# Decode attention with a gated MLP: K and V in 4 MB tiles, small operands as single rows, late weights in a K buffer, and h as a row

## The chip, the cores and the metric

The kernel runs on one core of one Trainium2 chip. The metric is device time in microseconds (us), the median of several executions. The time includes about 1.8 us beyond the span that the profile shows: the profiled execution of the old kernel took 193.56 us with a span of 191.8 us. The profile is of one execution. In it PE is the matrix engine (TensorE), PEld its weight loads, DVE the vector engine, ACT the scalar engine, SP the engine that issues most DMAs. This chapter calls an execution slow when it is over 1.5% above the fastest of the same kernel, and the comparisons of kernels use fast executions, except where it says so. The runs were made on several chips; each is compared with the old kernel on its own chip.

## The reference, cut to what matters

```
x = A_x                                             # [1, 1, 512], bf16
g = sigmoid((x * gate_w).sum(-1))
q = (x @ wq) as 32 heads of 128                     # wq: 4 MB
p = softmax(q . k_cache * 128**-0.5)                # 32 heads, 4096 keys: K 32 MB
a = (p . v_cache) as one row of 4096 @ wo           # V 32 MB, wo 4 MB
h = max(x @ w1 + b1, 0) ** 2                        # w1: 512 x 1376, 1.4 MB
b = h @ w2 + b2                                     # w2: 1376 x 512, 1.4 MB
out = g * a + (1 - g) * b                           # 512 numbers
```

One token reads 78 MB and computes little. Whatever order the work takes, those bytes have to cross the DMA engines.

## The kernel before

K and V come in sixteen tiles of 2 MB each, two heads to a tile, and every partition receives one run of 16 KB. K has four buffers, V three.

```
NP = 16;  NB = 64;  HB = NB // 2;  NK, NV = 4, 3;  PG = 4
k_t = A_k_cache ... .rearrange("(t p f) -> t p f", p=128, f=NB * 128)

d_wq = P.dma("sp", "wq", ... wbig <- wq)            # runs of 32 KB for each partition
d_x  = P.dma("act", "x",  ... x4   <- x  spread as [128, 4])    # 128 packets of 8 bytes
d_gw = P.dma("act", "gw", ... gw4  <- gate_w spread alike)
d_b1, d_b1r, d_b2 = ...                             # b1 in packets of 20 and 2 bytes
```

DVE multiplies half a K tile by q. Each key then has 128 products: PE, with an identity as its weights, adds their eight groups of 16, DVE adds up the 16 sums that are left, ACT takes the exponential, and PE multiplies by V:

```
for c in range(n):                                  # 8 matmuls for each half tile
    matmul(red[i % 2], ident, v[:, c, :, :], start=(c == 0), stop=(c == n - 1))
```

At the end the weights w1, wo, w2 arrive behind the last V tile, in this order. h is computed as columns, with w1 as the stationary operand, the one that is loaded into PE as weights (44 small matmuls of one column each), and everything is accumulated straight into one tile out_ps of PSUM, the memory that takes PE's results, so that after the last w2 matmul only one DVE copy and the store remain:

```
for j in range(32): to_out(wo_v[:, j, :], op_sb[:, j:j+1], ...)        # 64 matmuls of 256 columns
to_out(w2_r, ...)
for n, (lo, hi) in enumerate(W2_CUTS):              # ((0, 6), (6, 9), (9, 10)): three DMAs
    for j in range(lo, hi): done = to_out(w2_sb[:, j, :], hs[:, j:j+1], ...)
f = tensor_copy(fin, out_ps)
```

The softmax here doesn't subtract the row's maximum and nothing guards it: scores larger than these inputs give would overflow.

## Time and profile before

| | old kernel |
|---|---|
| median time | 194.76 us (194.51 to 194.91, 3 executions) |
| span of the profiled execution | 191.8 us |
| read from HBM | 78.32 MB |
| DMA rate from 20 to 170 us | 427 to 428 GB/s |
| last weights land (end of the last data packet in the trace) | 188.5 us |
| from there to the end of the span | 3.3 us |

The page of the old kernel: its first line, and the DMA share (tenths) and GB/s in 40 equal slices.

```profile
span 191.8 us, 1729 instructions
...
DMA  6999999999999999999999999999999999999991
GB/s 219 438 383 380 434 427 420 427 427 431 437 424 427 420 431 424 437 427 427 424 431 422 437 427 419 424 431 431 431 431 424 417 434 431 434 414 434 434 346 43
```

The engines that move data are busy from the second slice to the last but one. The third and fourth slices (383 and 380) are lower than the rest.

The table by windows of the old kernel: the window and its length, busy time and number of instructions for each engine, the granted PE clock (1.00 is full speed), the mean busy share of the 16 DMA engines, GB/s.

```profile
20.00:50.00 30.00, 17.50 (x87) 6.22 (x88) 19.97 (x18) 1.42 (x9) 0.00 (x0) 0.77 1.01 428
50.00:80.00 30.00, 20.11 (x126) 7.50 (x124) 19.90 (x14) 3.35 (x17) 0.00 (x0) 0.89 1.01 428
80.00:110.00 30.00, 19.01 (x112) 7.10 (x104) 17.26 (x12) 2.68 (x13) 0.00 (x0) 0.83 1.01 428
110.00:140.00 30.00, 19.47 (x104) 6.30 (x99) 17.35 (x12) 2.22 (x13) 0.00 (x0) 0.83 1.01 427
140.00:170.00 30.00, 18.74 (x104) 6.88 (x103) 17.17 (x12) 2.54 (x13) 0.00 (x0) 0.83 1.00 427
```

PE and DVE are busy for 17 to 20 of every 30 us, while the DMA share is full. Compute waits for data here, not the other way round. The Trainium skill, "DMA: Bandwidth & Descriptors", section Bandwidth, puts the ceiling of the path into SBUF at 435 GB/s; the 427 to 428 measured here is 98% of it.

The last pieces of the chain of waits of the old kernel, that is of the work that ended last, followed back from the end through what each piece waited for (start, length, what):

```profile
153.35 35.32 DMA w_sb<-in_B_w_dram
...
188.71 0.62 PE out_ps L354 x8
189.36 0.42 DVE fin L385
```

The last eight matmuls wait for their weights and then take 0.62 us. TensorE keeps up with the weights to the end.

One line of the list of DMA issues (size, and us from issue to landing):

```profile
x<-in_A_x_dram ACTq DMA_DIRECT2D x1, 1.0 KB, 12.8
```

One kilobyte takes 12.8 us, as long as the 4 MB of wq. The same page of the skill, section "Queues, rings and completion order", says that a DMA engine alternates between its queues packet by packet. The trace agrees: x lands together with wq, its tiny packets spread over wq's 10 us.

### The profile page before, as it was taken

How to read it: one execution, taken by the hardware profiler on the slowest of the kernel's cores; microseconds unless marked ns; L12 is line 12 of the kernel's file. 1: busy time of each engine (PE TensorE's matmuls, PEld its weight loads, DVE VectorE, ACT ScalarE, POOL GpSimd, SP SyncE). 2: the span in 40 equal slices, each digit the busy share in tenths (PEclk: the TensorE clock that was granted, in tenths of full speed). 3: DMA queues.
4: the chain of work that ended last, by engine and by line, in shares of the span. 5: the costliest groups of instructions: out<-in, count | busy, mean ns of one | idle time of the engine just before them, and what ended most of it. 6: DMA issues, size and time to landing. Idle time of an engine off the chain costs nothing.

```text
span 191.8 us, 1729 instructions
## 1 busy us (share of the span) xinstructions
PE 114.5 (60%) x721; PEld 45.6 (24%) x721; DVE 96.5 (50%) x83; ACT 17.3 (9%) x74; POOL 3.1 (2%) x13
## 2 busy tenths in 40 slices
PE   0009006998849493719573938484776654685974
PEld 0004002333212321303132312121232121223742
DVE  2000009699965655647473838382929191921300
ACT  2003100011102010101020101010111010102000
POOL 6000000000000000000000000000000000000000
PEclk9999955699996969985999696969697899579588
DMA  6999999999999999999999999999999999999991
GB/s 219 438 383 380 434 427 420 427 427 431 437 424 427 420 431 424 437 427 427 424 431 422 437 427 419 424 431 431 431 431 424 417 434 431 434 414 434 434 346 43
DMA packets 6285, 78.42 MB, mean 409 GB/s; under 512 B 1187, under 2 KB 1414, under 8 KB 1670
## 3 DMA queue, kind: packets, MB, share of 16 engines
q1 hardware_dynamic: 5732, 78.32, 97.0%
q8 instruction: 5, 0.08, 0.2%
q10 hardware_dynamic: 546, 0.01, 0.2%
q14 instruction: 2, 0.02, 0.0%
HBM read 78.32 MB, written 0.00 MB: 408 GB/s over the span
## 4 chain that ended last, share of the span: by engine, by line
DMA 77%; DVE 10%; PE 8%; SPq 2%; ACTq 1%; issue 1%
DMA Vt<-in_A_v_cache_dram 28%; DMA w_sb<-in_B_w_dram 18%; DMA Kt<-in_A_k_cache_dram 17%; DMA b_sb<-in_B_b_dram 13%; DVE prod L238 8%; PE red L252 5%; PE qps L279 3%; DVE S L259 2%; SPq L324 1%; SPq L322 0%; ACTq L164 0%; SPq L233 0%; PE out_ps L354 0%; DVE b_g L217 0%; ACTq L162 0%
## 5 line engine op out<-in xcount | busy, mean ns | idle before, releaser
L252 PE MATMUL red<-prod,ident 128*128 128x512 bf16 x256 | 74.1, 442 | 42.6 <-DVE prod L238 42.6
L238 DVE TENSOR_TENSOR prod<-Kt,qb 128x4096 bf16<-128x4096 bf16 x32 | 73.1, 2285 | 43.4 <-DMA Kt<-in_A_k_cache_dram 43.4
L252 PEld LDWEIGHTS red<-prod,ident 128*128 128x128 bf16 x256 | 25.2, 108 | 88.6 <-DVE prod L238 50.9
L259 DVE TENSOR_REDUCE S<-red 128x32 f32<-128x512 f32 x32 | 22.0, 686 | 8.5 <-PE red L252 8.4
L279 PE MATMUL qps<-Vt,E 128*32 128x512 bf16 x256 | 22.0, 476 | 4.7 <-DMA Vt<-in_A_v_cache_dram 3.1
L267 ACT ACTIVATE E<-S 64x64 bf16<-64x64 f32 x32 | 8.8, 274 | 131.7 <-DVE S L259 131.5
L197 PE MATMUL qps<-wbig,xb 128*64 128x512 bf16 x32 | 5.0, 480 | 14.0 <-DVE xb L188 14.0
L279 PEld LDWEIGHTS qps<-Vt,E 128*32 128x32 bf16 x256 | 6.4, 109 | 20.6 <-issue 16.7
L220 PE MATMUL out_ps<-b_g,ones 1*64 1x256 f32 x4 | 1.1, 656 | 9.8 <-DVE b_g L217 9.8
L188 DVE COPY xb<-x 128x512 bf16<-128x512 bf16 x1 | 0.4, 427 | 11.4 <-DMA x<-in_A_x_dram 11.4
L197 PEld LDWEIGHTS qps<-wbig,xb 128*64 128x64 bf16 x32 | 2.2, 135 | 16.3 <-DVE xb L188 14.0
L354 PE MATMUL out_ps<-wbig,op_sb 128*1 128x256 bf16 x64 | 5.3, 335 | 1.3 <-DMA wbig<-in_A_wo_dram 1.3
L267 ACT ACTIVATION_READ_ACCUMULATOR E<-S 64x1 f32 x32 | 5.9, 185 | 0.0
L217 DVE TENSOR_SCALAR b_g<-b_sb,gate 1x512 f32<-1x512 bf16 x1 | 0.5, 475 | 8.5 <-DMA b_sb<-in_B_b_dram 8.5
L291 PEld LDWEIGHTS o_ps<-pick,acc_sb 128*128 128x128 f32 x32 | 4.1, 191 | 1.6 <-ACT acc_sb L286 1.2
L291 PE MATMUL o_ps<-pick,acc_sb 128*128 128x8 f32 x32 | 3.9, 249 | 0.7 <-ACT acc_sb L286 0.7
L385 DVE CAST fin<-out_ps 128x256 bf16<-128x256 f32 x1 | 0.4, 425 | 7.2 <-PE out_ps L354 7.2
L354 PEld LDWEIGHTS out_ps<-wbig,op_sb 128*1 128x1 bf16 x64 | 3.1, 101 | 3.2 <-DMA wbig<-in_A_wo_dram 1.6
L201 ACT ACTIVATE qb<-qps 128x512 bf16<-128x512 f32 x4 | 2.4, 598 | 12.3 <-PE qps L197 12.3
L286 ACT ACTIVATE acc_sb<-qps 128x512 f32<-128x512 f32 x4 | 2.4, 597 | 10.2 <-PE qps L279 10.2
L210 DVE TENSOR_SCALAR gate<-gate 128x1 f32<-128x1 f32 x1 | 0.2, 154 | 5.9 <-ACT gate L209 5.9
L220 PEld LDWEIGHTS out_ps<-b_g,ones 1*64 1x64 f32 x4 | 0.3, 199 | 9.9 <-DVE b_g L217 9.9
(40 smaller groups left out, 18.8 us busy)
## 6 DMA issues: line engine op xcount, KB each, us to landing
Kt<-in_A_k_cache_dram SPq DMA_DIRECT2D x16, 2048.0 KB, 31.6
Vt<-in_A_v_cache_dram SPq DMA_DIRECT2D x16, 2048.0 KB, 27.3
wbig<-in_A_wq_dram SPq DMA_DIRECT2D x1, 4096.0 KB, 12.6
wbig<-in_A_wo_dram SPq DMA_DIRECT2D x2, 2048.0 KB, 32.2
w_sb<-in_B_w_dram SPq DMA_DIRECT2D x1, 1376.0 KB, 25.3
w_sb<-in_B_w_dram SPq DMA_DIRECT2D x1, 768.0 KB, 34.8
w_sb<-in_B_w_dram SPq DMA_DIRECT2D x1, 384.0 KB, 35.3
w_sb<-in_B_w_dram SPq DMA_DIRECT2D x1, 128.0 KB, 34.1
```

The costliest lines, as they stand in the source:

```text
L197: last = P.add("pe", lambda e, c=c, half=half, t=t: e.matmul(qps[c % 2][64 * half:64 * half + 64, :], xb[:, t, 0:64], wq_v[:, t, 4 * c:4 * ...
L201: q_done.append(P.add("act", lambda e, c=c: e.activation(qb[:, 4 * c:4 * c + 4, :], qps[c % 2][:, :].rearrange("p (g d) -> p g d", d=128), ...
L220: P.add("pe", lambda e, hh=hh: e.matmul(out_ps[64 * hh:64 * hh + 64, :], ones[0:1, 0:64], b2_g[0:1, 256 * hh:256 * hh + 256], start=True, ...
L238: prods[p, half] = P.add("dve", lambda e: e.tensor_tensor(prod[:, i % 2, :].rearrange("p (b d) -> p b d", d=128), Kt[:, p % NK, half * HB ...
L252: pe_sums[i] = P.add("pe", lambda e, c=c: e.matmul(red[i % 2][:, :, :], ident[:, :], v[:, c, :, :], start=(c == 0), stop=(c == n - 1)), pr ...
L259: sums[i] = P.add("dve", lambda e: e.tensor_reduce(S[:, p % 2, half * HB:(half + 1) * HB], red[i % 2][:, :, :], AX.X, ALU.add), pe_sums[i] ...
L267: exps[p] = P.add("act", lambda e, q=q, hh=hh: e.activation(E[q, k, :, 8 * k + hh:8 * k + hh + 7:2], S[q, p % 2, :].rearrange("p (g b) -> ...
L279: pvs[p] = P.add("pe", lambda e, g=g, c=c: e.matmul(acc[32 * c:32 * c + 32, :], E[:, k, g, :], Vt[:, p % NV, g * 512:(g + 1) * 512], start ...
L286: copies[G] = P.add("act", lambda e: e.activation(acc_sb[:, :], acc[:, :], ACT.Copy), pvs[p], picked.get(G - 1))
L291: picked[G] = P.add("pe", lambda e, b=b: e.matmul(o_ps[:, 2 * PG * G:2 * PG * (G + 1)], acc_sb[:, 128 * b:128 * b + 128], pick[:, b, :], s ...
L324: d_w2r = P.dma("sp", "w2r", lambda e: e.dma_start(w2_r[:, :], B_w2[128 * NJ:F, :]))
L354: done = P.add("pe", lambda e, hh=hh: e.matmul(out_ps[64 * hh:64 * hh + 1, :], v, w[:, 256 * hh:256 * hh + 256], start=False, stop=last, s ...
```

## The change

The change means to make the DMA stream more even (fewer and larger packets, no tiny ones), to spare weight loads on PE, and to pack the tail. Its core, cut:

```diff
-    NP = 16
-    NB = 64
-    NK, NV = 4, 3
-    PG = 4
+    NQ = 8
+    NB = 128
+    NC = 4
+    WO_CUTS = ((0, 16), (16, 24), (24, 32))
+    PG = 2
...
-        w1_sb = sb("w1_sb", [128, 4, F], bf16)      # and w2_sb, w2_r: own buffers
-        Kt = sb("Kt", [128, NK, NB * 128], bf16)
-        Vt = sb("Vt", [128, NV, NB * 128], bf16)
+        Kt = sb("Kt", [128, 2, NB * 128], bf16)
+        Vt = sb("Vt", [128, 2, NB * 128], bf16)
+        late, at = Kt[:, 0, :], 0                   # w1, w2, rows of h: in K slot 0
...
-        d_x = P.dma("act", "x", lambda e: e.dma_start(x4[:, :], x_t))
+        d_x = P.dma("act", "x", lambda e: e.dma_start(xrow[:, :], x_t))
+        # x reaches the partitions by four one-row matmuls; gate, b1 likewise rows
...
+            if c == 0 or c == 2:
+                P.add("pe", lambda e: e.ldweights(ident[:, :]), i1)
+            # then 16 matmuls (two quarters of a tile) that hold the identity, each without a load
...
         d_w1 = P.dma("sp", "w1", lambda e: e.dma_start(
-            w1_sb[:, :, :].rearrange("p t n -> p (t n)"), w1_t))
+            w1_sb.rearrange("p t n -> p (t n)"), w1_t), k_free)
...
+        for t in range(4):                          # h as a row: x holds, w1 moves
+            P.add("pe", lambda e, t=t: e.ldweights(xb[:, t, :]))
+            for lo, hi in chunks:                   # 3 chunks of up to 512 columns
+                hm = ... held(e, h_ps[:, lo:hi], xb[:, t, :], w1_sb[:, t, lo:hi], ...)
+        ha, hb = ...                                # two DVE passes over one row of 1376
...
-        for j in range(32):
-            to_out(wo_v[:, j, :], op_sb[:, j:j + 1], False, t2, d_wo[j // 16])
+        project_wo(0)                               # in all three parts 32 matmuls, into four column groups
+        ...  11 one-row matmuls turn h into columns  ...
+        project_wo(1)
+        wo_done = project_wo(2)
+        wc = P.add("act", ... wo_sb <- wo_ps)
...
+            if n == 0:                              # behind the first part of w2
+                for hh in range(2):
+                    P.add("pe", ... out_ps += ones(fp32) x wo_sb(fp32) ..., wc)
```

Two K slots and two V slots of 4 MB replace seven of 2 MB. On PE the order behind the last V tile is now: PV, gather, denominators, h, wo, transposes of h, wo, w2 with the fp32 sum of the four column groups in between.

## The prediction

> **What bounds the kernel now.** The DMA stream. The profile's header shows 78.32 MB read from HBM at 408 GB/s over a span of 191.8 us. The table by windows gives 427 to 428 GB/s and a DMA share of 1.00 to 1.01 in every 30 us stretch from 20 to 170 us, while DVE and PE are busy some 60 to 65% there. The chain of waits is 77% DMA. The Trainium skill, "DMA: Bandwidth & Descriptors", section Bandwidth, gives a fabric ceiling of 435 GB/s; the trace agrees that 427 is near a limit. The change moves the same bytes, so the steady state can yield under 2%. Outside it: from 1 to 20 us the stream averages about 375 GB/s (some 2.3 us lost), and after the last weights land (188.7) come 0.62 us PE, 0.42 us DVE and the output's DMA.
>
> **What changes, costed.**
>
> 1. K and V in 4 MB tiles: rows of 32 KB instead of 16 KB, 16 K/V transfers instead of 32. In the trace's DMA packets a 16 KB packet takes 611 ns (quiet) to 615 ns (with compute); the 32 KB packets of wq, already laid out like that, take 1214 ns undisturbed. That is 8 ns per 32 KB, plus 9 ns per completion write: about 73 ns per 4 MB, times 16, is 1.2 us saved, all on the critical path.
>
> 2. Small loads as rows: 546 tiny packets become about ten. x landed 12.8 us after issue, b2 held the first product until 29.3 us; both vanish. But K had four slots, the stream did not stop for it, and packets next to those of b1 took 611 ns, so most of this is off the path. Estimate: 0.2 to 0.8 us.
>
> 3. Two 4 MB slots instead of four and three of 2 MB. A K tile costs DVE about 4 x (2.28 + 0.69) = 11.9 us against 19.6 us of transfers per K+V pair, so the next load is issued some 15 us before the queue would run dry. No starvation, even at half TensorE clock (32 sums x 450 ns + 4.2 us of PV = 18.6 us per pair). Zero.
>
> 4. Held identity: some 250 weight loads fewer (25 us PEld, overlapped). Zero on the path.
>
> 5. Tail: h as a row costs 15 matmuls of up to 512 columns (about 3 us at full clock), two one-row DVE passes (estimated 1.5 us each) and 11 small transposes; wo shrinks from 64 to 32 matmuls, but adds a copy and two fp32 matmuls placed behind the first w2 part. 16 us of weights still stream after the last V, which hides this at full or mixed clock. The fp32 matmuls (1.12 us at half clock in the trace for two) delay the end about 0.4 us; a clock of 0.5 through the whole tail would add up to 5 us.
>
> Sum: -1.2 - 0.5 + 0.4, about -1.4 us: 193.3 us.
>
> **Prediction.** 193.3 us, 8 in 10 between 191.3 and 195.2. Chances: faster by over 2% 0.07, within 2% 0.88, slower by over 2% 0.05.
>
> **Right if** the windows from 20 to 170 us show about 430 GB/s; 32 KB packets take about 1220 ns; x lands within 5 us; first product at about 22 us; PE waits for w2 near the end (no backlog); last landing 1.5 to 2 us earlier, and half a microsecond more after it.
>
> **Wrong if** 32 KB packets are slowed by compute more than 16 KB ones; the DMA share falls below 1.00 between tiles (starvation); the start's loss belonged to the small packets wholly (then about 191.5); or PE is still busy with h and wo when w2 lands, at a low clock (then 195 and over).

## The result, and the profile after

The changed kernel ran at 194.69 us median of four executions, but no execution took that: they were 196.31, 193.08, 192.86 and 196.64 us. The old kernel beside it had 194.82 us. The ratio is 0.9908, with a 95% interval of 0.9884 to 0.9932. Ratios are computed as the mean time of one kernel's fast executions over that of the other's of the same rounds, so they are not quite the ratio of the medians that are quoted. By the ratio it is faster by 0.9%, which counts as the same within 2%. With the slow half of its executions counted in, nothing is gained.

The first profile was of a slow execution. First what went well in it. The windows of the changed kernel, slow execution:

```profile
20.00:50.00 30.00, 18.53 (x96) 1.16 (x36) 21.99 (x15) 1.88 (x8) 0.00 (x0) 1.00 1.00 431
50.00:80.00 30.00, 16.02 (x77) 0.95 (x34) 17.86 (x13) 4.36 (x17) 0.00 (x0) 0.77 0.99 424
80.00:110.00 30.00, 19.67 (x125) 2.71 (x76) 16.36 (x12) 2.48 (x9) 0.00 (x0) 0.89 1.02 436
110.00:140.00 30.00, 17.98 (x89) 1.84 (x43) 19.57 (x14) 3.77 (x16) 0.00 (x0) 0.77 1.01 434
140.00:170.00 30.00, 18.46 (x124) 2.62 (x82) 15.29 (x12) 4.41 (x17) 0.00 (x0) 0.86 0.98 422
```

Single windows scatter by a few GB/s, as packets of 32 KB at a border are counted on one side, but their mean is 429; with every packet spread over its duration, the changed kernel moves 430.9 GB/s from 20 to 170 us in all four of its profiles, the old one 427.2. Weight loads (the third column of numbers) fell from 6 to 7.5 us to 1 to 2.7 us for every 30 us. The stream did not starve with two slots. The end of the trace's last data packet moved from 188.5 to 186.3 us: the weights are there 2.2 us earlier. And yet the span is longer, 194.5 instead of 191.8 us. The chain of waits of the changed kernel from its last V tile on, slow execution:

```profile
146.41 23.37 DMA Vt<-in_A_v_cache_dram
...
169.92 3.63 PE qps L178 x30
173.57 0.60 ACT acc_sb L319
...
174.22 1.92 PE o_ps L324 x8
...
177.91 4.58 PE big L180 x12
...
188.67 1.63 PE out_ps L416 x12
190.31 0.85 PE out_ps L442 x3
191.16 0.88 PE out_ps L416 x7
192.06 0.48 DVE fin L446
```

After the V tile (146.41 + 23.37 = 169.8) no DMA stands in this chain any more. For 22 us it is PE work and what hangs on it: PV (3.63), the gather (1.92), h (4.58, and in pieces left out here two DVE passes over its row of 1.45 and 1.59 and its transposes of 0.81), at last w2. The last part of w2 had landed at 186.3, and its matmuls ran at 191.16. In the old kernel the chain was with a DMA until 3 us before the end.

A profile in the fast state (the run after_look2 below), its end of the chain:

```profile
149.87 35.79 DMA Kt<-in_B_w_dram
...
185.71 1.49 PE out_ps L416 x12
187.20 0.85 PE out_ps L442 x4
188.05 0.87 PE out_ps L416 x8
188.94 0.48 DVE fin L446
```

Here PE waits for w2, as in the old kernel. From the start of the first w2 part to the last matmul it needs 3.2 us; the old kernel needed 1.6 us from 187.77 on. The difference is the fp32 sum, 0.85 us, and half clock, at which the w2 matmuls take 1.49 + 0.87 = 2.36 instead of 1.6 us (a wait of 0.4 us for the last part included). What full clock would give is seen in w1_before_v6 below, whose chain there has 0.89 + 0.45 = 1.34 us for 22 of these matmuls and 0.47 us for the fp32 sum.

### The profile page after: what moved, and what is told of

Same layout as the page of the kernel before. It is cut to its first block, busy times and chain, and to the rows that moved or that the text cites. A ratio compares the mean times of both kernels' runs of the same rounds, so it can differ in the third digit from the quotient of the medians.

```text
span 194.5 us, 1358 instructions
## 1 busy us (share of the span) xinstructions
PE 114.0 (59%) x672; PEld 19.0 (10%) x424; DVE 100.0 (51%) x84; ACT 20.5 (11%) x73; POOL 3.8 (2%) x17
## 4 chain that ended last, share of the span: by engine, by line
DMA 61%; PE 20%; DVE 17%; issue 0%; ACT 0%; SPq 0%
DMA Kt<-in_A_k_cache_dram 49%; DVE prod L271 13%; PE big L180 12%; DMA Vt<-in_A_v_cache_dram 12%; DVE S L291 2%; PE qps L178 2%; PE big L178 2%; PE out_ps L416 1%; PE o_ps L324 1%; PE wo_ps L178 1%; DVE Kt L397 1%; DVE Kt L395 1%; PE out_ps L442 0%; PE misc L427 0%; ACT acc_sb L319 0%
## 5 line engine op out<-in xcount | busy, mean ns | idle before, releaser
L180 PE MATMUL big<-prod,ident 128*128 128x512 bf16 x256 | 74.9, 451 | 58.5 <-DVE prod L271 58.5
L291 DVE TENSOR_REDUCE S<-big 128x32 f32<-128x512 f32 x32 | 22.0, 686 | 8.0 <-PE big L180 8.0
L299 ACT ACTIVATE E<-S 32x128 bf16<-32x128 f32 x32 | 15.0, 470 | 99.9 <-DVE S L291 99.5
L178 PE MATMUL qps<-Vt,E 128*32 128x512 bf16 x128 | 9.3, 443 | 4.1 <-DMA Vt<-in_A_v_cache_dram 4.1
L178 PE MATMUL big<-Vt,E 128*32 128x512 bf16 x128 | 7.6, 380 | 0.0
L299 ACT ACTIVATION_READ_ACCUMULATOR E<-S 32x1 f32 x32 | 7.6, 236 | 0.0
L324 PEld LDWEIGHTS o_ps<-acc_sb,pick 128*32 128x32 f32 x32 | 3.6, 124 | 38.0 <-issue 36.2
L324 PE MATMUL o_ps<-acc_sb,pick 128*32 128x128 f32 x32 | 5.1, 312 | 0.7 <-ACT acc_sb L319 0.7
L178 PEld LDWEIGHTS big<-Vt,E 128*32 128x32 bf16 x128 | 3.0, 96 | 24.9 <-issue 22.2
L180 PE MATMUL big<-Kt,xb 128*128 128x512 bf16 (+1 forms) x12 | 4.7, 578 | 0.0
```

The source lines that it names most:

```text
L178: return e.matmul(o, w, m, start=start, stop=stop, skip_group_check=True, tile_position=(0, col) if cols < 128 else None)
L180: return e.add_instruction(mybir.InstMatmult(name=nc.get_next_instruction_name(), engine=e.engine, ldweights=False, start_tensor_calc=star ...
L291: sums[i] = P.add("dve", lambda e: e.tensor_reduce(S[:, p % 2, c * HB:(c + 1) * HB], red[i % 2], AX.X, ALU.add), pe_sums[i], exps.get(p - 2))
L299: exps[p] = P.add("act", lambda e, q=q, h=h: e.activation(E[q, k, :, 16 * k + h:16 * k + h + 13:4], S[q, p % 2, :].rearrange("p (g b) -> p ...
L324: picked[G] = P.add("pe", lambda e, b=b: e.matmul(o_ps[32 * G:32 * G + 32, :], pick[:, b, :], acc_sb[:, 128 * b:128 * b + 128], start=(b = ...
```

## The experiments

The lead of one stream over another is found by adding up the bytes of the DMA packets in the traces up to a given time (instruction packets left out, a packet under way counted in part), and dividing the difference by 428 GB/s.

### The changed kernel again (after_again, after_look, after_look2)

No edit. My theory was that both states have the same stream, and that what differs is the TensorE work left at the end and the clock it gets. The rival was that the slow state loses its time in the stream.

> The changed kernel again, unaltered, for its states and a profile of its fast state. Theory (tail): its last weights land at about 186.4 us of the span in every run, and the difference between fast (191.2) and slow (194.5) is made after that by TensorE work still queued up at a low granted clock; a fast profile shows DMA landing within 0.3 us of 186.4 and a higher clock between 170 and 190. Rival (stream): the slow state loses its 3.3 us in the DMA stream (share under 0.95 somewhere between 20 and 180), and a fast profile shows the last landing about 3 us earlier than 186.4. Times: mixed, 193 and 196.5.

> The changed kernel unaltered, one more look for a profile in its fast state. Theory: in a fast profile the last landing is again near 186.4 us and the half-clock stretches after 165 us cover less of the end than the 13.6 and 6.8 us in the slow profiles; span about 191. If it is slow again, it should repeat 194.5 with the same half-clock stretches.

> The changed kernel unaltered, another look for a profile of its fast state: last landing 186.2 to 186.5 us, span about 191, and of the 21 to 22 us from the last V to the end fewer at half clock than the 18.8 us of the slow profile (about 12 if each microsecond at half clock costs half a microsecond of work that would have been done).

Measured: 196.33, 192.97, 192.88, 196.51, 196.41, 192.97 us (after_again, ratio 0.9923), 196.64 (after_look) and 193.24 us (after_look2). With the first four executions, six of twelve lie at 196.3 to 196.6 and six at 192.9 to 193.2. Averaged over all six executions, fast and slow, after_again took 194.68 us, against 194.43 us for the eleven of the old kernel beside it. Three profiles are slow (spans 194.5, 194.5, 194.9) and after_look2 is fast (191.4). Their last landings are 186.3, 186.5, 186.5 and, in the fast one, 186.5 us. So the rival falls: the stream is the same in both states. The clock is not. Windows of 3.4 us behind the last V tile, slow execution:

```profile
170.40:173.80 3.40, 3.12 (x32) 0.97 (x24) 0.00 (x0) 0.23 (x1) 0.00 (x0) 0.50 1.00 426
173.80:177.20 3.40, 2.98 (x12) 2.02 (x13) 0.48 (x2) 0.36 (x1) 0.00 (x0) 0.50 0.97 410
177.20:180.60 3.40, 3.40 (x10) 0.41 (x3) 0.10 (x1) 0.00 (x0) 0.00 (x0) 0.50 1.00 412
...
187.40:190.80 3.40, 3.40 (x30) 1.85 (x24) 0.00 (x0) 0.60 (x1) 0.00 (x0) 0.50 0.00 0
```

The same windows of the fast execution (after_look2):

```profile
170.40:173.80 3.40, 2.79 (x32) 0.92 (x23) 0.00 (x0) 0.57 (x1) 0.00 (x0) 0.53 1.03 438
173.80:177.20 3.40, 3.32 (x20) 1.63 (x16) 0.58 (x2) 0.03 (x1) 0.00 (x0) 0.96 0.98 414
177.20:180.60 3.40, 2.36 (x27) 0.73 (x21) 2.01 (x3) 0.00 (x0) 0.00 (x0) 1.00 1.00 415
...
187.40:190.80 3.40, 1.50 (x12) 0.72 (x8) 0.48 (x1) 0.00 (x0) 0.00 (x0) 0.50 0.00 0
```

The third number from the right, the granted clock, tells the states apart: 0.50 for three windows in a row against 0.53, then 0.96 and 1.00. The mean clock of the whole span does not (0.842 slow, 0.839 fast). The Trainium skill, "TensorE: Matmul & The Clock Gate", Part 1, says that the clock is gated by activity in windows of 3413 ns that run freely and do not restart with a kernel. The trace agrees with the size: the half-clock stretches of these runs last 3.4, 6.8, 10.2, 13.6 or 20.5 us. It would also explain why two executions of one kernel differ, by where the window borders happen to fall. The clock records go some way with it. In all profiles of the changed kernel and of own_identity the last PV starts between 169.8 and 170.1 us. The half-clock stretch around it began at 168.6, 168.5 and 169.3 us in the three slow profiles and lasted 13.6 us, and it began at 170.6 us in the fast one, at 169.7 us in more_code (fast too), and lasted 3.4 us; in own_identity, which lies between the states, it began at 171.0 and lasted 10.2 us. So the borders do fall differently in the two states. But these are six profiles, and no run here set the phase, so that it decides the state is an explanation and not a finding.

### w1_before_v6: h out of the time behind the last V

w1 is loaded before the last two V tiles, and h is computed before PV of the last two:

```diff
+            if p == NQ - 1:                 # w1's DMA, put ahead of V6 in the SP queue
+                d_w1 = P.dma("sp", "w1", ..., k_free)
...
+        <bias and h matmuls, ha, hb: moved up to here>
+        pv(NQ - 2)
         pv(NQ - 1)
         gather(NQ // PG - 1)
```

> w1 is loaded before the last two V tiles, and h is computed while TensorE waits for them. Theory (tail): about 6 us of TensorE work and 3.2 us of DVE work leave the time after the last V; last landing stays within 0.3 us of 186.4, the chain behind it shrinks from 8.1 us (slow) to about 4 us or less, both states merge near 192 us or below, none over 194. Rival (stream, or the out DMA): the slow state near 196.5 stays in about half of the runs.

Measured: 191.76 to 193.65 us, median 192.99, ratio 0.9921. The slow state near 196.5 is gone from all six executions. The last landing is 186.5 us, and 3.9 us follow it (8.2 in the slow profile). The fast executions of the changed kernel were not beaten. The reason is on the chain of this run:

```profile
146.62 26.68 DMA Vt<-in_A_v_cache_dram
...
173.43 3.63 PE qps L178 x32
...
184.31 1.74 PE wo_ps L178 x16
186.05 0.89 PE out_ps L422 x14
186.94 0.47 PE out_ps L448 x4
187.41 0.45 PE out_ps L422 x8
```

Putting w1 first moves the last V from 169.8 to 173.3 us. TensorE still leads the chain from there to the end, at half clock until 185.8 us, but its last matmul ends at 187.9 us, 1.4 us behind the last landing, where it was 5.7 us in the slow profile. The expectation held for the states, and was about one microsecond too hopeful about the time.

### h_skipped: the h matmuls taken away

```diff
-        for t in range(4):
-            P.add("pe", lambda e, t=t: e.ldweights(xb[:, t, :]))
-            for lo, hi in chunks:
-                hm = P.add("pe", ... held(e, h_ps[:, lo:hi], xb[:, t, :], w1_sb[:, t, lo:hi], ...)
```

The bias matmuls wait for w1 in their place. The result is wrong (relative error 0.19).

> The changed kernel without the 12 matmuls of h with w1 (wrong result on purpose, everything else kept): 4.6 us of TensorE work at half clock, 2.5 us at full, leave the time after the last V. Theory (TensorE queue at the end): the last landing stays at 186.4 us, the slow profile shrinks from 194.5 to about 190, the times lie at 191 to 192 us with a spread under 1.5 us, no pair of states 3.5 us apart. Rival (the slow state belongs to the stream or to the host of the run): times still fall in two groups 3 us apart.

Measured: 192.89 to 193.68 us, one group. Its profile has half clock from 167.9 to 188.4 us, a longer stretch than in any slow profile, and still a span of 191.1 us, because PE waits for weights again (timeline of h_skipped: start, busy, what, in brackets the idle time before and what ended it):

```profile
183.21 0.14 PEld L178 LDWEIGHTS wo_ps<-wbig,op_sb 128*32 128x32 bf16 x8 [0.94 <-DMA wbig<-in_A_wo_dram]
...
185.39 1.04 PEld L411 LDWEIGHTS out_ps<-Kt,hs 128*64 128x64 bf16 x12 [1.08 <-DMA Kt<-in_B_w_dram]
```

This settles the slow state. Half clock alone does not make it; half clock together with h behind the last V does. The times were 1 to 2 us above what I expected, since I had left out that the w2 matmuls and the fp32 sum at half clock follow the landing: the span ends 5.0 us after it here too.

### rows_16k: two loads for each tile

```diff
-            d_k.append(P.dma("sp", ..., Kt[:, p % 2, :] <- k_t[p]))
+            for hf in range(2):             # K, and V alike
+                part_ = P.dma("sp", ..., Kt[:, p % 2, hf*8192:hf*8192+8192] <- k_t[p][:, same])
+            d_k.append(part_)
```

> Each 4 MB K or V tile loaded by two DMAs of 16 KB rows. Theory (packet size): the lead that the changed kernel gains on the old one between 20 and 165 us (1.3 us) is gone, so the last landing moves from 186.4 to about 187.6; the start up to 20 us stays as in the changed kernel (packets of K0 at 611 ns). Rival: if the slow spell of the old kernel at 13 to 16.4 us (16 KB packets of up to 805 ns) comes from 16 KB rows, it returns here. Total time only partly follows, as the end waits for TensorE: 0 to 1.2 us longer in like states.

Measured: 197.45, 197.49, 194.19, 194.50 us, ratio 0.9996. The lead over the old kernel's stream was:

| lead over the old stream, us, at | 13 us | 16 us | 20 us | 25 us | 165 us |
|---|---|---|---|---|---|
| changed kernel | 0.23 | 0.99 | 1.15 | 1.22 | 2.43 |
| rows_16k | 0.24 | 0.98 | 1.12 | 1.17 | 1.27 |
| tiny_loads (below) | 0.09 | 0.81 | 0.80 | 0.57 | 1.57 |

The start is untouched, and from 20 to 165 us the lead grows by 0.15 instead of 1.28 us. The windows of rows_16k show the old rate again:

```profile
80.00:110.00 30.00, 19.04 (x126) 2.70 (x76) 16.62 (x12) 2.48 (x9) 0.00 (x0) 0.87 1.01 428
110.00:140.00 30.00, 18.18 (x88) 1.84 (x43) 18.86 (x13) 3.77 (x16) 0.00 (x0) 0.77 1.01 429
```

The last landing is 187.8 us, 1.3 to 1.5 later than in the changed kernel. The larger tiles are worth 1.2 us of stream, as predicted. The run doesn't part the packet's size from the number of transfers. The old kernel's slow spell at 13 to 16 us did not come back with 16 KB rows: those packets took 611 ns.

### tiny_loads: the 480 tiny packets added again

```diff
+        t1_ = P.dma("act", "tx", ... x4 <- x spread as [128, 4])      # nobody reads these tiles
+        t2_ = P.dma("act", "tg", ... gw4 <- gate_w spread alike)
+        t3_ = P.dma("act", "tb", ... b1_x[:, 0:NJ] <- b1 in 20 byte pieces)
+        t_end = P.dma("act", "tr", ... b1_x[0:FT, NJ] <- the rest in 2 byte pieces)
```

> The 480 tiny packets of the old kernel (x, gate and two of b1 spread over partitions) added again into tiles nobody reads, behind the new rows. Theory (tiny packets delay the stream): the lead of about 0.9 us at 16 us over the old kernel falls to 0.2 or less, and packets near 13 to 16 us take over 700 ns per 16 KB; the last landing moves from 186.4 to about 187.2. Rival (16 KB rows, or chance, made that slow spell): the stream at 20 us is within 0.2 us of the changed kernel.

Measured: 196.97, 193.75, 193.83, 194.34 us, ratio 0.9976. The lead at 165 us is 0.86 us smaller than in the changed kernel (the table above), and the last landing is 186.8 us, 0.3 to 0.5 later. The windows of the start, tiny_loads:

```profile
2.00:20.00 18.00, 4.44 (x38) 1.89 (x39) 3.30 (x11) 2.43 (x4) 2.57 (x10) 1.00 0.97 406
20.00:50.00 30.00, 18.57 (x96) 1.12 (x36) 21.98 (x15) 1.89 (x8) 0.00 (x0) 1.00 1.00 425
```

And the changed kernel (after_look2):

```profile
2.00:20.00 18.00, 4.45 (x38) 1.90 (x39) 3.30 (x11) 2.43 (x4) 2.57 (x10) 1.00 0.97 415
20.00:50.00 30.00, 19.53 (x96) 1.16 (x36) 21.98 (x15) 1.90 (x8) 0.00 (x0) 0.83 1.00 431
```

So the tiny packets do delay the stream, by about 0.6 us within the first 25 us. But they did it elsewhere: the slow packets were at 18 to 22 us (up to 669 ns for each 16 KB, as a mean over 16 packets), not at 13 to 16 us (up to 805 ns) as in the old kernel, and at 16 us the lead had not fallen to the 0.2 us that I expected. Slow spells came only in the two kernels with tiny packets, and mostly beside the ones of 8 bytes; why a spell starts where it does stays open. The two edits do not give back the whole lead either: of 2.43 us at 165 us rows_16k takes 1.16 and tiny_loads 0.86, and about 0.4 us is left without an explanation.

### own_identity: a weight load for each summing matmul

```diff
-            if c == 0 or c == 2:
-                P.add("pe", lambda e: e.ldweights(ident[:, :]), i1)
-                pe_sums[i] = ... held(e, red[i % 2], ident[:, :], v[:, k, :, :], ...)
+                pe_sums[i] = ... e.matmul(red[i % 2], ident[:, :], v[:, k, :, :], ...)
```

> The changed kernel with one weight load of the identity for each of the 256 summing matmuls, as the old kernel had. If the held identity is worth nothing, as predicted: the stream up to 165 us and the two states (193 and 196.5) stay. Rival: the added loads lengthen the sums (over 451 ns mean each) or shift the clock, and the mean moves by over 1 us.

Measured: 195.21, 196.56, 193.53, 193.15, 192.92 us, ratio 0.994. Its weight loads take 43.7 us instead of 19.0, the sums 446 ns instead of 451, the lead at 165 us is 2.40 instead of 2.43 us, and the last landing is 186.2. The held identity shows no effect on the stream, and none on the time beyond the noise (interval of the ratio 0.9887 to 0.9993, of after_again 0.9896 to 0.995). This run also gave a state in between, which by the rule of 1.5% counts among the fast ones: its profile (span 193.4) has 16.4 us of half clock between the last V and the final DVE instruction, against 18.7 in the slow profile and 8.0 in the fast one. The 195.21 and the 193.53 show that the two states are not two fixed values, but depend on how much of the end the clock is at half.

### tail_reordered, w2_two_cuts, w2r_aside: towards a better end

tail_reordered adds three moves to w1_before_v6: the last V comes in two halves, the transposes of h stand between their PVs, and the fp32 sum stands before w2.

```diff
-        pv(NQ - 1)
+        pv(NQ - 1, 0, NG // 8)              # first half of the last V
+        <11 transposes of h>
+        pv(NQ - 1, NG // 8, NG // 4)
...
+        <fp32 sum of wo: out_ps += ones x wo_sb>     # before all parts of w2
         for n, (lo, hi) in enumerate(W2_CUTS):
```

> A version meant to beat both: w1 before V6, h before PV of V6, the last V in two halves with the transposes of h between, and the fp32 sum of wo before w2. Theory: TensorE has under 1 us of work left when the last weights land (186.4 to 186.6), so the span is 189.5 to 190.3 in any clock phase: 191.2 to 192.2 us, ratio to the old kernel about 0.985, spread under 1 us. Rival (something else sets the end): no better than w1_before_v6, mean near 192.8.

Measured: 192.40 to 193.01 us, median 192.48, ratio 0.9904. All six executions lie within 0.6 us. PE has work left in the end, but only w2's own (timeline of tail_reordered):

```profile
185.13 1.12 PE L446 MATMUL out_ps<-Kt,ones 128*64 128x256 f32 x4 [0.34 <-ACT Kt L443]
...
186.04 2.07 PE L434 MATMUL out_ps<-Kt,hs 128*64 128x256 bf16 x20
...
188.15 0.48 DVE L454 SCALAR_TENSOR_TENSOR fin<-b_sb,gate,out_ps 128x256 bf16<-128x256 bf16 x1 [9.54 <-PE out_ps L434]
```

The twenty w2 matmuls take 2.07 us, at half clock until 187.7 us, starting 0.3 us before the last landing (186.3). I had expected under 1 us of work there, and a ratio of 0.985.

Both of the others start from tail_reordered. w2_two_cuts joins the last two parts of w2. w2r_aside cuts w2 in two elsewhere, moves its 96 rows of 1 KB to the other queue and the fp32 sum between the parts. The cut lines alone:

```diff
-    W2_CUTS = ((0, 6), (6, 9), (9, 10))
+    W2_CUTS = ((0, 6), (6, 10))             # w2_two_cuts
+    W2_CUTS = ((0, 7), (7, 10))             # w2r_aside
```

> tail_reordered with the last two parts of w2 (rows of 3 KB and 1 KB) as one part of 4 KB rows. Between 185.0 and 186.3 us of the changed kernel's stream the DMA share is only about 0.3, while 1 KB packets, taking 46 ns each, make up the queue. Theory (packets of 1 KB leave their engine idle between them, some 0.1 us each): the last landing moves from 186.3 to 185.4 to 185.7; the time falls by 0 to 0.5 us, as at half clock TensorE is now the later one. Rival (the low share is the engines ending unevenly, or the last completions): the last landing stays at 186.2 or later.

> tail_reordered with w2 in two parts of 7 KB and 3 KB rows, the 96 rows of 1 KB of w2_r loaded on the other queue, interleaved with the last K and V tiles, and the fp32 sum of wo between the parts of w2. Theory: last landing about 185.0 us, TensorE done by 187.4 at half clock (188.1 before), span about 189.8, median about 191.7 us, ratio about 0.986 to the old kernel. Rival: the small rows cost as much beside the large ones (last landing not under 185.7), median 192.4 as before.

Measured: w2_two_cuts 192.06 to 192.99 us, median 192.51, ratio 0.9893, last landing 186.5 us: it did not move, and the theory that 1 KB packets leave gaps falls. w2r_aside 193.25, 191.76, 191.73, 193.15, 191.74, 191.95 us, median 191.86, ratio 0.9885 (interval 0.984 to 0.9931), last landing 186.4 us. It has the best median of all, though the intervals of the three (0.9873 to 0.9934 for tail_reordered, 0.985 to 0.9936 for w2_two_cuts) overlap too far to rank them, and its mean of all six executions is 192.26 us against 194.56 for the old kernel beside it. Its gain did not come the way I expected, since the landing stayed. The profile is of one of its two executions near 193.2: PE is at half clock from 174.9 to 188.6 us, and the span ends 5.1 us behind the last landing. No profile of an execution near 191.8 was kept, so that the clock makes this difference too is not shown.

### more_code: 1200 empty instructions

In the six profiles examined for it (one of the old kernel, two of the changed one, three of its variants, this run among them) the 16 engines' completions of one K or V tile lie 0.4 to 0.7 us apart until the first 16 KB instruction packet (at 51 us in the changed kernel, at 45 us in the old one), and 1.3 to 2.2 us apart from then on. Empty instructions were meant to bring such packets earlier.

```diff
+        for _ in range(1200):
+            P.add("pool", lambda e: e.nop())
```

> The changed kernel with 1200 empty instructions on the idle GpSimd queue, near its start. In all profiles of the changed kernel the 16 engines finish each load within 0.5 us of each other until the first 16 KB instruction packet (51 us, taking 1.1 us), and 1.4 to 2.2 us apart from then on, up to the last weights. Theory (an instruction packet puts the one DMA engine that carries it behind for good, and the last landing waits for the laggard): more instruction packets appear early, the completions of the second load (near 22 us) are already over 1 us apart, and the last landing is at 186.5 us or later. Rival (the spread comes from K and V tiles waiting to be issued, or from compute): no change before 51 us, and the spread there stays 0.5 us.

The profile has 1358 instructions and four instruction packets, just as before: the empty instructions made none. Nothing was tested, and the theory stays a coincidence in time. The run: 192.93 us, span 191.1, half clock from 169.7 to 173.1 and from 183.4 us on, 8.7 us up to the last DVE instruction.

## Why the prediction was right or wrong

The time was right for the fast executions: 193.3 us was forecast, and they took 192.9 to 193.2 us. The median, 194.69, also lies within 191.3 to 195.2, and the change is within 2%, but that the median lies there is luck: it is the middle between two fast and two slow executions, and with three slow ones of four it would have been over 196. The prediction listed "PE is still busy with h and wo when w2 lands, at a low clock (then 195 and over)" among the signs that it is wrong, and this is what the slow half did. Point by point:

1. *4 MB tiles, 1.2 us.* Right. The packets of 32 KB took 1214 ns (median), and rows_16k gives back 1.16 us of lead at 165 us.
2. *Tiny loads, 0.2 to 0.8 us.* Right in kind, slightly too small. tiny_loads gives back 0.86 us of lead at 165 us, though only 0.3 to 0.5 us of it is left at the last landing. x was used by PE at 2.6 us, and the first product started at 22.7 us.
3. *Two slots don't starve.* Right: the windows from 20 to 170 us average 429 GB/s; and the lead at 165 us is 2.33 to 2.47 us in ten profiles of the changed kernel and of variants that leave these tiles alone until then (w2r_aside, with its small rows beside the last tiles, has 2.0).
4. *Held identity, zero.* Right as far as the noise lets one see (own_identity).
5. *Tail.* This is the step that failed in size. "The fp32 matmuls ... delay the end about 0.4 us", and, under what would show it right, "PE waits for w2 near the end (no backlog)". From the last landing to the end of the span the old kernel's profile has 3.3 us, the fast profile of the changed one 4.9, the slow one 8.2. In the fast state the term is 1.6 us: 0.85 us for the fp32 sum and 0.8 us for w2 at half clock, where I had counted on a mixed or full clock. In the slow state it is 5 us. I had named that case ("a clock of 0.5 through the whole tail would add up to 5 us") and given it little weight; it came in half of all executions. w1_before_v6, h_skipped and tail_reordered each remove it. The prediction took the 16 us of weights behind the last V to hide this work; in the slow profile it took 22 us. The new form of h has a large part in that: as columns in the old kernel, h took 4.0 us from its first matmul to its last DVE instruction (178.2 to 182.2 us, at half clock); as a row it has 4.58 + 1.45 + 1.59 + 0.81 = 8.4 us of the slow profile's chain. The changed kernel with h as columns was not run.

So where did the gain go? The weights arrive 2.0 to 2.2 us earlier. Some 1.6 us of it is spent again behind the last landing in the fast profile, more than all of it in the slow one. One thing doesn't add up exactly: between the profiles the fast span is 0.4 to 0.6 us shorter than the old one, but the ratios of the fast executions (0.9923 and 0.9908) stand for 1.5 to 1.8 us. The old kernel's profile was one of its fastest executions (193.56 us, where its executions reached from 193.46 to 196.06), with full clock from 183.9 to 190.8 us. A typical execution of the old kernel, which I have no profile of, takes some 0.8 to 0.9 us more: the mean span of the 34 that the record lists with their spans is 192.6 us. Those of up to 192.1 us have a mean clock of 0.847 to 0.857, those of 192.8 us and over one of 0.831 to 0.842, so the clock goes along with it; that the clock at the end is the cause is likely but not shown.

## What to carry to other kernels

When a change makes a saturated stream faster, ask what is on the other engines at the moment the stream ends. Here the weights came 2 us earlier, but in the slow state the serial work behind the last V tile took 22 us, longer than the weights still had to stream, and then it and not the stream set the end. Cost the tail at the lowest granted clock that the trace shows, not at the mean, and move everything that doesn't depend on the last data ahead of it (w1 before the last V left the last landing at 186.5 us and took away a state that was 3.5 us slower). And where single executions of one kernel fall into groups, get a profile of each group before explaining the median: here the median was a time that no execution took.

## What the Trainium skill lacked or had wrong

- "TensorE: Matmul & The Clock Gate", Part 1, calls the ramp penalty under 1% of a typical kernel's span and advises against fitting a model to a certain number of slow matmuls. In this kernel the clock at the end goes along with more: spans of 194.5 and 191.4 us (1.6%) for the same program, with last landings 0.2 us apart.
- The same part says that the clock is released after at least one busy window of about 3.4 us. The windows shown above do not start at the clock's own borders. Counted from these (168.6 us on, slow profile), PE is busy for 2.08, 2.70, 3.40 and 3.40 of 3.40 us, and the clock stays at 0.50 until the end of the fourth; in the fast profile one window with 2.71 us (from 170.6) was enough. PE's busy time is modelled by the profiler. What counts as busy there the page doesn't say.
- "DMA: Bandwidth & Descriptors" names at least 1 MiB for each transfer as the rule for maximum bandwidth. It lacks that the step from 2 MB with 16 KB a partition to 4 MB with 32 KB still counts: 614 ns for a 16 KB packet against 1214 ns for a 32 KB one (medians), 1.2 us of stream between 20 and 165 us.
- It lacks what packets of 8 bytes do to bulk packets beside them: single spells of up to 805 (old kernel) instead of 611 ns for 16 KB, some 0.6 us by 25 us for 480 packets (tiny_loads), at places that differ from kernel to kernel.
- No page of those used here says what a 16 KB instruction packet (1.0 to 1.1 us on one DMA engine) does to the stream. After the first one, the engines' completions of every load were 1.3 to 2.2 us apart instead of 0.4 to 0.7. The one run meant to test it tested nothing.
